# Where a two-stage network meets its second stage: GpSimd's low parts in smaller pieces, a second buffer for words, sums of tokens in half steps

## The chip, the cores and the metric

One core of a Trainium2 chip runs the whole program. The metric is the device time of one execution in microseconds. TensorE (PE), VectorE (DVE), ScalarE (ACT), GpSimd (POOL) and SyncE's DMA queue (SP) work side by side and wait for each other by semaphores.

## The reference

All in float32: `x = attention(q, k, v, p)` over 8 batches of 576 tokens and 512 channels; `x = elu(x @ w_in) @ w_out` with 2048 hidden columns; and last, the part that this case is about:

```python
def _moe2_ref(x, w_a, w_b, w_out):
    a = x @ w_a          # 4608 x 512 by 512 x 1536
    b = x @ w_b
    return (a * b @ w_out).astype(np.float32)
```

The weights arrive as float64 words and are made into float32 on the chip.

## The kernel before, in words

**Numbers.** A float32 product is made of three passes. Each operand is split in a high part (a cast on ACT, L82, L707, L790) and a low part (the operand less its high part, a two-input subtraction: DVE in L83, GpSimd in L708 and L791).

**First phase.** For each batch of 576 tokens PE does 32 steps, `m1_block` (L621): the six matmuls of `l1` (L453) and the twelve of `l2` (L475, two steps behind). Between them `act1` (L459) takes the result through ACT (L461, L462), DVE (L465, the step's `gf`), ACT (L467, high part) and DVE (L469, low part). Other work is put between these instructions at a time counted in half steps: `put(t, fn)` notes it and `run_until` (L517) issues it, at an even time ahead of L465 and at an odd time ahead of L469. T7 is the time at which the last batch begins, so T7 + 34 lies in its 18th step. In this phase PE, DVE and ACT keep the order in which the program is written. `x2_out` (L483) copies a half batch's result from four PSUM banks to two staging tiles (`x2s`, two banks each, one copied by ACT and one by DVE) and stores them to DRAM (L494). It comes after step 17 and after the last step of each batch. The banks are free for the next half's `l2` when they are copied.

**Second phase.** Six groups `g` of 768 tokens, twelve rounds `f` of 128 hidden columns each. By a scheme that needs seven products instead of eight, `l3` (L812) makes seven products of sums of weight blocks (tile `e2`, seven blocks with two parts) with sums of token blocks (tiles `s1` to `s7`) in three PSUM banks A, B, C, in the order A1, B6, C5, A2, B7, C3, B4. Each is six matmuls at L802. B7 waits until DVE has read B6 (L827), B4 until DVE has read B7 (L832). `l4` (L846) then does nine matmuls of the round before. Here only PE keeps the written order; the compiler's scheduler fixes that of the other engines when the program is built.

**The border.** The weight sums of group 0 are made on the spot. `e_load_words` (L690) loads the float32 words of w_a and w_b of one `f` into two tiles with the tag `wmag`, of which there are two, so a new pair waits until the pair before has been read. `e_make` (L696) makes four block sums on DVE (L702 to L705, tile `wc`), casts seven blocks on ACT in three instructions (512, 256 and 1024 columns) and takes seven low parts on GpSimd in three instructions of the same sizes (L708), then stores the tile to DRAM for the other groups (`ed`, L709). `e2` has two buffers, so the ACT casts for `f + 2` start when round `f` is through. `o_load` (L786) loads and splits a block of w_out, with one GpSimd instruction of 512 columns (L791). `x_load` (L717) loads four token tiles with eight DMAs, and `s_steps` (L733) makes the parts s1 to s7 and four sums of 768 columns in eight steps, put at T7 + 45, 47, ... 59. For the later groups the steps come at the end of the group before.

**Buffers.** The pool `stage` has five buffers with the tag `wst`: the token tiles, their sum `x2s1`, the weight sums `wc` and the staging tiles `x2s` all come from them, in the order in which the program asks.

```python
put(T7 + 14, e_make, 0)
put(T7 + 20, e_load_words, 1)
put(T7 + 30, e_make, 1)
put(T7 + 36, e_load_words, 2)
put(T7 + 36, x_load, 0)
for n in range(8):
    put(T7 + 45 + 2 * n, s_step, 0, n)
```

Of the kernel before, what the change touches and what calls it, by code (L numbers as in the profile page):

```python
# [20 lines left out]
P = 128  # L21
# [4 lines left out]
def program(tc, q, k, v, p, w_in, w_out, w_a, w_b, w_out2, out):  # L26
# [21 lines left out]
    HT = 384  # L48
# [12 lines left out]
    with ctx:  # L61
# [628 lines left out]
        def e_load_words(f):  # L690
            for kind in "ab":
                t = stage.tile([P, 512], F32, tag="wmag", name=f"wl{kind}{f}", bufs=2)
                nc.sync.dma_start(t, wf[kind, f])
                wst2[kind, f] = t

        def e_make(f):  # L696
# [9 lines left out]
            for i, n, src in ((0, 2, a.rearrange("p (n x) -> p n x", n=2)), (2, 1, b[:, None, h2]), (3, 4, c)):  # L706
                nc.scalar.copy(e[:, i:i + n, 0, :], src)  # L707
                nc.gpsimd.tensor_tensor(e[:, i:i + n, 1, :], src, e[:, i:i + n, 0, :].bitcast(F32), op=ALU.subtract)  # L708
# [19 lines left out]
        def s_part(g, i, src):  # L728
            s = p2.tile([P, 2, 2 * HT], F32R, tag=f"s{i}", name=f"s{i}_{g}")
            split(s[:, 0, :], s[:, 1, :], src)  # L730
            ss[i] = s.rearrange("p h (k n) -> p h k n", k=2)

        def s_steps(g):  # L733

            flat = lambda t, kh: xs[g, t, kh].rearrange("p k n -> p (k n)")
            tt = nc.vector.tensor_tensor

            def first():
                s_part(g, 1, flat(0, 0))
                xs[g, "s1"] = stage.tile([P, 2 * HT], F32, tag="wst", name=f"x2s1_{g}")  # L740
                tt(xs[g, "s1"], flat(1, 0), flat(1, 1), op=ALU.add)

            def second():
                tt(flat(1, 0), flat(0, 0), flat(1, 0), op=ALU.subtract)
                tt(flat(0, 0), xs[g, "s1"], flat(0, 0), op=ALU.subtract)

            def seventh():
                tt(flat(0, 1), flat(0, 1), flat(0, 0), op=ALU.subtract)
                s_part(g, 3, flat(0, 1))

            return [
                first,
                second,
                lambda: s_part(g, 6, flat(0, 0)),
                lambda: s_part(g, 5, xs[g, "s1"]),
                lambda: s_part(g, 2, flat(0, 1)),
                lambda: s_part(g, 7, flat(1, 0)),
                seventh,
                lambda: s_part(g, 4, flat(1, 1)),
            ]  # L760

        def s_step(g, n):
            if n == 0:
                ss["steps"] = s_steps(g)
            ss["steps"][n]()
# [6 lines left out]
        put(T7 + 36, x_load, 0)  # L772
        for n in range(8):
# [153 lines left out]
```

## Time and profile before

| what | value |
|---|---|
| time, median of 3 runs | 1645.46 us (1644.58 to 1646.12) |
| the profiled execution's own time | 1646.58 us |
| its span, first to last instruction | 1644.8 us |
| mean granted TensorE clock | 0.979 of full speed |
| PE busy | 1569.8 us, 95% of the span |
| DVE busy | 1025.1 us, 62% |
| ACT busy | 717.0 us, 44% |
| POOL busy | 168.8 us, 10% |

In a timeline row the first number is the start from the span's start, the second the time from the start of the first to the end of the last instruction of the row; a bracket gives the idle time of the engine before it and what ended that. An instruction that waits for something after it has been taken up is shown as longer. The last batch's steps lie at about 717 to 799 us, group 0's rounds at 800 to 926 us.

### The profile page before, as it was taken

The page shows a single profiled execution, that of the slowest core. Times are in us where ns is not written, and L with a number is a line of the kernel's source. Part 1 is how long each engine was busy: PE and PEld are TensorE (multiplying, and loading weights), DVE is VectorE, ACT ScalarE, POOL GpSimd, SP SyncE. Part 2 cuts the span into 40 slices and gives each one's busy share as a digit, 9 for nine tenths or more (in the row PEclk, how much of TensorE's full clock was granted, in tenths as well). Part 3 has the DMA queues.
Part 4 walks back from the last instruction along what each step waited for, and adds up shares of the span by engine and source line. Part 5 has one row for each costly group of instructions (what it writes and reads, how often), then busy time and mean ns, then how long its engine had stood idle before and what let it go on. Part 6 is the DMA issues. An engine that isn't in the chain of part 4 may idle for free.

```text
span 1644.8 us, 27465 instructions
## 1 busy us (share of the span) xinstructions
PE 1569.8 (95%) x10824; PEld 1438.4 (87%) x10824; DVE 1025.1 (62%) x2054; ACT 717.0 (44%) x1579; POOL 168.8 (10%) x122
## 2 busy tenths in 40 slices
PE   5488999999999999999889999999999999999999
PEld 3376998989898999999788899989989989998997
DVE  6988676777777676755588735634545453563452
ACT  6675666666666666665433312312222221231211
POOL 3321010000000100011364100000000000000000
PEclk7599999999999999999999999999999999999999
DMA  8755334525262624114366745535445554552541
GB/s 253 179 162 129 105 102 103 131 53 142 76 158 69 154 80 110 47 66 144 117 229 233 268 148 185 221 136 207 180 166 188 213 201 147 184 208 107 211 180 39
DMA packets 214785, 247.95 MB, mean 151 GB/s; under 512 B 150144, under 2 KB 180864, under 8 KB 205440
## 3 DMA queue, kind: packets, MB, share of 16 engines
q1 hardware_dynamic: 214656, 246.19, 46.3%
q8 instruction: 85, 1.39, 0.3%
q14 instruction: 44, 0.36, 0.1%
HBM read 194.64 MB, written 51.51 MB: 150 GB/s over the span
## 4 chain that ended last, share of the span: by engine, by line
PE 79%; DVE 6%; issue 4%; ACT 3%; DMA 3%; POOL 3%; SPq 2%; DVEq 0%; POOLq 0%; ACTq 0%
PE x2a L475 21%; PE o L846 17%; PE B L802 12%; PE h L453 10%; PE C L802 8%; PE A L802 8%; POOL e L708 2%; SPq L164 1%; POOL wo L791 1%; DMA wst_i<-in_moe_w_in_dram 1%; DVE gr L469 1%; DVE gf L465 1%; PE pp L301 1%; ACT gr L467 0%; DVE wr L83 0%
## 5 line engine op out<-in xcount | busy, mean ns | idle before, releaser
L475 PE MATMUL x2a<-gr,wout 128*128 128x288 f32 x3072 | 466.2, 300 | 10.3 <-DVE gr L469 6.4
L475 PEld LDWEIGHTS x2a<-gr,wout 128*128 128x128 f32 x3072 | 424.1, 190 | 51.6 <-issue 12.3
L846 PE MATMUL o<-wo,c 128*128 128x512 f32 x1296 | 309.2, 393 | 0.0
L846 PEld LDWEIGHTS o<-wo,c 128*128 128x128 f32 x1296 | 243.7, 189 | 48.2
L802 PE MATMUL B<-s,e 128*128 128x384 f32 x1296 | 262.8, 337 | 11.1 <-DVE u L827 5.3
L453 PE MATMUL h<-a,wr 128*128 128x288 f32 x1536 | 251.2, 299 | 16.9 <-DVE gf L465 8.6
L453 PEld LDWEIGHTS h<-a,wr 128*128 128x128 f32 x1536 | 220.8, 191 | 26.4 <-DVE gf L465 12.9
L802 PEld LDWEIGHTS B<-s,e 128*128 128x128 f32 x1296 | 228.2, 189 | 15.2 <-DVE u L827 7.8
L802 PE MATMUL A<-s,e 128*128 128x384 f32 x864 | 174.7, 336 | 1.0 <-ACT p L825 1.0
L802 PE MATMUL C<-s,e 128*128 128x384 f32 x864 | 173.9, 335 | 0.0
L465 DVE SCALAR_TENSOR_TENSOR gf<-ge,h 128x288 f32<-128x288 f32 x256 | 113.7, 445 | 85.8 <-ACT ge L462 83.1
L467 ACT CAST gr<-gf 128x288 fp32r<-128x288 f32 x256 | 110.4, 432 | 129.8 <-DVE gf L465 128.7
L802 PEld LDWEIGHTS A<-s,e 128*128 128x128 f32 x864 | 153.8, 188 | 7.2 <-ACT p L825 1.3
L469 DVE TENSOR_TENSOR gr<-gf,gr 128x288 fp32r<-128x288 f32 x256 | 131.5, 514 | 34.4 <-ACT gr L467 32.3
L802 PEld LDWEIGHTS C<-s,e 128*128 128x128 f32 x864 | 152.8, 189 | 0.0
L82 ACT CAST c<-u 128x384 fp32r<-128x384 f32 x72 | 36.8, 512 | 230.3 <-DVE u L835 230.3
L461 ACT ACTIVATE ge<-h 128x288 f32<-128x288 f32 x256 | 104.5, 409 | 74.0 <-PE h L453 73.3
L832 DVE TENSOR_TENSOR v<-p,B 128x384 f32<-128x384 f32 x72 | 39.8, 552 | 143.3 <-PE B L802 143.2
L462 ACT ACTIVATE ge<-ge 128x288 f32<-128x288 f32 x256 | 113.8, 445 | 7.6
L827 DVE TENSOR_TENSOR u<-p,B 128x384 f32<-128x384 f32 x72 | 39.7, 552 | 105.1 <-PE B L802 105.1
L825 ACT COPY p<-A 128x384 f32<-128x384 f32 x72 | 34.7, 482 | 120.2 <-PE A L802 120.1
L829 ACT COPY p<-C 128x384 f32<-128x384 f32 x72 | 34.7, 482 | 102.2 <-PE C L802 102.2
(342 smaller groups left out, 1449.1 us busy)
## 6 DMA issues: line engine op xcount, KB each, us to landing
e<-ed SPq DMA_DIRECT2D x60, 1792.0 KB, 7.1
ed<-e SPq DMA_DIRECT2D x12, 1792.0 KB, 6.4
x2d<-x2s SPq DMA_DIRECT2D x32, 288.0 KB, 2.4
out_dram<-osb SPq DMA_DIRECT2D x36, 256.0 KB, 2.0
v<-in_v_dram SPq DMA_DIRECT2D x8, 1024.0 KB, 7.8
wst_i<-in_moe_w_in_dram SPq DMA_DIRECT2D x16, 512.0 KB, 5.4
wst_o<-in_moe_w_out_dram SPq DMA_DIRECT2D x16, 512.0 KB, 4.5
kst<-in_k_dram SPq DMA_DIRECT2D x112, 72.0 KB, 2.5
```

Of the source, the lines that this page charges most:

```text
L82: nc.scalar.copy(hi, src)
L453: nc.tensor.matmul(t[:, :HS], w[:, wi, o * P:(o + 1) * P], x[:, xi, :], start=(n == 0), stop=(n == 5))
L461: nc.scalar.activation(e, t[:, :HS], AF.Relu, scale=-1.0)
L462: nc.scalar.activation(e, e, AF.Exp, scale=-1.0)
L465: nc.vector.scalar_tensor_tensor(g, e, -1.0, t[:, :HS], op0=ALU.add, op1=ALU.max)
L467: nc.scalar.copy(gr[:, 0, :], g)
L469: nc.vector.tensor_tensor(gr[:, 1, :], g, gr[:, 0, :].bitcast(F32), op=ALU.subtract)
L475: nc.tensor.matmul(acc[d][:, :HS], wout_r[f][:, wi, d * P:(d + 1) * P], gr[:, xi, :], start=(first and n == 0), stop=(last and n == 2),)
L802: nc.tensor.matmul(bank[:, :HT], es[f][:, E_OF[i], wi, k * P:(k + 1) * P], ss[i][:, xi, k, :], start=(first and n == 0), stop=(n == 5), sk ...
L827: nc.vector.tensor_tensor(u, p1, pB, op=ALU.add)
L832: nc.vector.tensor_tensor(v, p1, pB, op=ALU.add)
L846: nc.tensor.matmul(acc, cr[:, xi, t * P:(t + 1) * P], wo[f][:, wi, :], start=(f == 0 and n == 0), stop=(f == NF2 - 1 and n == 2),)
```

## The change

Five edits. (1) `e_make`'s three GpSimd instructions become seven of 256 columns, and `o_load`'s one becomes two of 256. (2) The word pairs of f = 3, 5, 7, 9, 11 go into one tile of the tag `wst` instead of two of `wmag`. (3) Word pairs are asked for a round earlier: pair 3 at T7 + 62, pair f + 4 in round f. (4) `x_load` of group 0 moves from T7 + 36 to T7 + 28. (5) The eight steps on tokens become 22 half steps of 384 columns, one in each half step from T7 + 40 to T7 + 61, in another order of the parts; for the later groups the same 22 stand where the eight stood.

```diff
@@ -688,8 +688,9 @@
         xs, ss = {}, {}
 
         def e_load_words(f):
-            for kind in "ab":
-                t = stage.tile([P, 512], F32, tag="wmag", name=f"wl{kind}{f}", bufs=2)
+            both = stage.tile([P, 2, 512], F32, tag="wst", name=f"wl{f}") if f % 2 and f > 1 else None
+            for n, kind in enumerate("ab"):
+                t = stage.tile([P, 512], F32, tag="wmag", name=f"wl{kind}{f}", bufs=2) if both is None else both[:, n, :]
                 nc.sync.dma_start(t, wf[kind, f])
                 wst2[kind, f] = t
 
@@ -705,7 +706,10 @@
             nc.vector.tensor_tensor(c[:, 3, :], a[:, h2], c[:, 2, :], op=ALU.subtract)
             for i, n, src in ((0, 2, a.rearrange("p (n x) -> p n x", n=2)), (2, 1, b[:, None, h2]), (3, 4, c)):
                 nc.scalar.copy(e[:, i:i + n, 0, :], src)
-                nc.gpsimd.tensor_tensor(e[:, i:i + n, 1, :], src, e[:, i:i + n, 0, :].bitcast(F32), op=ALU.subtract)
+                for x in range(n):
+                    nc.gpsimd.tensor_tensor(
+                        e[:, i + x, 1, :], src[:, x, :], e[:, i + x, 0, :].bitcast(F32), op=ALU.subtract
+                    )
             nc.sync.dma_start(ed[f], e.bitcast(F32))
             es[f] = e
 
@@ -725,43 +729,39 @@
                     done += n
                 xs[g, t, kh] = x
 
-        def s_part(g, i, src):
-            s = p2.tile([P, 2, 2 * HT], F32R, tag=f"s{i}", name=f"s{i}_{g}")
-            split(s[:, 0, :], s[:, 1, :], src)
-            ss[i] = s.rearrange("p h (k n) -> p h k n", k=2)
-
         def s_steps(g):
 
-            flat = lambda t, kh: xs[g, t, kh].rearrange("p k n -> p (k n)")
             tt = nc.vector.tensor_tensor
-
-            def first():
-                s_part(g, 1, flat(0, 0))
-                xs[g, "s1"] = stage.tile([P, 2 * HT], F32, tag="wst", name=f"x2s1_{g}")
-                tt(xs[g, "s1"], flat(1, 0), flat(1, 1), op=ALU.add)
-
-            def second():
-                tt(flat(1, 0), flat(0, 0), flat(1, 0), op=ALU.subtract)
-                tt(flat(0, 0), xs[g, "s1"], flat(0, 0), op=ALU.subtract)
-
-            def seventh():
-                tt(flat(0, 1), flat(0, 1), flat(0, 0), op=ALU.subtract)
-                s_part(g, 3, flat(0, 1))
-
-            return [
-                first,
-                second,
-                lambda: s_part(g, 6, flat(0, 0)),
-                lambda: s_part(g, 5, xs[g, "s1"]),
-                lambda: s_part(g, 2, flat(0, 1)),
-                lambda: s_part(g, 7, flat(1, 0)),
-                seventh,
-                lambda: s_part(g, 4, flat(1, 1)),
-            ]
+            x11, x12, x22, x21 = (xs[g, t, kh] for t, kh in ((0, 0), (0, 1), (1, 1), (1, 0)))
+            s1 = stage.tile([P, 2, HT], F32, tag="wst", name=f"x2s1_{g}")
+            steps = []
+
+            def combine(dst, a, b, op):
+                steps.extend(lambda k=k: tt(dst[:, k, :], a[:, k, :], b[:, k, :], op=op) for k in range(2))
+
+            def part(i, src):
+                ss[i] = p2.tile([P, 2, 2, HT], F32R, tag=f"s{i}", name=f"s{i}_{g}")
+                steps.extend(lambda k=k: split(ss[i][:, 0, k, :], ss[i][:, 1, k, :], src[:, k, :]) for k in range(2))
+
+            part(1, x11)
+            combine(s1, x21, x22, ALU.add)
+            part(5, s1)
+            combine(x21, x11, x21, ALU.subtract)
+            combine(x11, s1, x11, ALU.subtract)
+            part(6, x11)
+            part(7, x21)
+            part(2, x12)
+            combine(x12, x12, x11, ALU.subtract)
+            part(3, x12)
+            part(4, x22)
+            return steps
+
+        NS = 22
 
         def s_step(g, n):
             if n == 0:
                 ss["steps"] = s_steps(g)
+                assert len(ss["steps"]) == NS
             ss["steps"][n]()
 
         put(T7 + 4, e_load_words, 0)
@@ -769,9 +769,10 @@
         put(T7 + 20, e_load_words, 1)
         put(T7 + 30, e_make, 1)
         put(T7 + 36, e_load_words, 2)
-        put(T7 + 36, x_load, 0)
-        for n in range(8):
-            put(T7 + 45 + 2 * n, s_step, 0, n)
+        put(T7 + 28, x_load, 0)
+        for n in range(NS):
+            put(T7 + 40 + n, s_step, 0, n)
+        put(T7 + 62, e_load_words, 3)
         m1_block(B - 1)
         while pend:
             run_pend()
@@ -788,7 +789,8 @@
             nc.sync.dma_start(t, wf["o", f])
             w = p4.tile([P, 2, 512], F32R, tag=f"wo{f}", name=f"wo{f}", bufs=1)
             nc.scalar.copy(w[:, 0, :], t)
-            nc.gpsimd.tensor_tensor(w[:, 1, :], t, w[:, 0, :].bitcast(F32), op=ALU.subtract)
+            for x in (slice(0, 256), slice(256, 512)):
+                nc.gpsimd.tensor_tensor(w[:, 1, x], t[:, x], w[:, 0, x].bitcast(F32), op=ALU.subtract)
             wo[f] = w
 
         def bank2(tag, name, bufs):
@@ -869,8 +871,8 @@
                         o_load(f)
                         if f + 2 < NF2:
                             e_make(f + 2)
-                        if f + 3 < NF2:
-                            e_load_words(f + 3)
+                        if f + 4 < NF2:
+                            e_load_words(f + 4)
                     c1[f], c2[f] = l3(g, f)
                     if g and f + 2 < NF2:
                         e_load(f + 2, g)
@@ -882,7 +884,7 @@
                 if g + 1 < NG:
                     for f in range(2):
                         e_load(f, g + 1)
-                    for n in range(8):
+                    for n in range(NS):
                         s_step(g + 1, n)
                 acc2 = bank2("A", f"o{g}_{TT}", 2)
                 for f in range(NF2 - 1):
```

## Rows read from the trace of the kernel before

**Rows 1.** Page, part 2: busy tenths of PE in 40 equal slices (41 us each).
```profile
PE   5488999999999999999889999999999999999999
```

**Rows 2.** Timeline of PE, 740 to 925 us: start, length, instructions, idle time before.
```profile
759.03 1.88 PE L475 MATMUL x2a<-gr,wout 128*128 128x288 f32 x12 [0.44 <-ACT x2s L492]
...
779.26 1.75 PE L475 MATMUL x2a<-gr,wout 128*128 128x288 f32 x12
...
781.65 0.29 PE L475 MATMUL x2a<-gr,wout 128*128 128x288 f32 x1
782.20 1.75 PE L475 MATMUL x2a<-gr,wout 128*128 128x288 f32 x11 [0.26 <-DVE gr L469]
...
793.88 0.29 PE L475 MATMUL x2a<-gr,wout 128*128 128x288 f32 x1
...
817.83 2.29 PE L802 MATMUL B<-s,e 128*128 128x384 f32 x6 [3.60 <-DVE v L832]
...
823.50 1.20 PE L802 MATMUL A<-s,e 128*128 128x384 f32 x6
...
832.87 1.23 PE L802 MATMUL A<-s,e 128*128 128x384 f32 x6
...
878.52 1.23 PE L802 MATMUL A<-s,e 128*128 128x384 f32 x6
...
883.35 1.31 PE L802 MATMUL B<-s,e 128*128 128x384 f32 x6 [0.47 <-DVE u L827]
...
888.67 1.23 PE L802 MATMUL A<-s,e 128*128 128x384 f32 x6
```

**Rows 3.** Windows: from, to, length, busy of PE, PEld, DVE, ACT, POOL; PEclk, DMA share, GB/s.
```profile
815.00:820.00 5.00, 2.17 (x7) 2.17 (x8) 4.36 (x8) 0.00 (x0) 2.03 (x2) 0.63 1.03 367
...
927.00:955.00 28.00, 28.00 (x125) 23.17 (x124) 9.85 (x15) 4.03 (x7) 0.00 (x0) 1.00 0.45 159
```

**Rows 4.** Timeline of VectorE (DVE), 740 to 925 us, columns as in rows 2.
```profile
780.82 0.96 DVE L83 TENSOR_TENSOR s<-x2s,s 128x768 fp32r<-128x768 f32 x1 [1.24 <-ACT s L82]
...
815.49 0.42 DVE L702 TENSOR_TENSOR wc<-wlb,wla 128x256 f32<-128x256 f32 x1 [3.40 <-DMA wlb<-wfb]
...
879.00 1.15 DVE L83 TENSOR_TENSOR c<-u,c 128x384 fp32r<-128x384 f32 x1 [1.13 <-ACT c L82]
880.07 2.75 DVE L83 TENSOR_TENSOR c<-w,c 128x384 fp32r<-128x384 f32 x1
```

**Rows 5.** Timeline of GpSimd (POOL), 740 to 925 us, columns as in rows 2.
```profile
834.46 2.40 POOL L708 TENSOR_TENSOR e<-wc,e 128x1024 fp32r<-128x1024 f32 x1 [0.57 <-ACT e L707]
...
878.99 0.75 POOL L708 TENSOR_TENSOR e<-wlb,e 128x256 fp32r<-128x256 f32 x1
879.68 2.73 POOL L708 TENSOR_TENSOR e<-wc,e 128x1024 fp32r<-128x1024 f32 x1
```

**Rows 6.** Timeline of ScalarE (ACT), 740 to 925 us, columns as in rows 2.
```profile
779.62 0.43 ACT L467 CAST gr<-gf 128x288 fp32r<-128x288 f32 x1 [0.97 <-DVE gf L465]
779.96 0.83 ACT L82 CAST s<-x2s 128x768 fp32r<-128x768 f32 x1
780.69 0.40 ACT L461 ACTIVATE ge<-h 128x288 f32<-128x288 f32 x1
781.13 0.44 ACT L462 ACTIVATE ge<-ge 128x288 f32<-128x288 f32 x1
...
878.46 0.51 ACT L82 CAST c<-u 128x384 fp32r<-128x384 f32 x1
```

**Rows 7.** Chain that ended last, 740 to 960 us: start, length, what.
```profile
760.84 6.50 DMA x2d<-x2s
```

**Rows 8.** Timeline of SyncE's DMA queue (SP), 740 to 925 us, columns as in rows 2.
```profile
757.56 0.32 SPq L709 DMA_DIRECT2D ed<-e  x1
```

**Rows 9.** Page, part 6: DMA issues, KB each, us to landing.
```profile
ed<-e SPq DMA_DIRECT2D x12, 1792.0 KB, 6.4
x2d<-x2s SPq DMA_DIRECT2D x32, 288.0 KB, 2.4
```

## The prediction

> **What bounds the kernel now.** I read the page first: PE is at 8 or 9 tenths in every slice after the first three, and only slices 19 to 21, some 780 to 900 us, fall off [rows 1]. That is the border which the change touches. PE's timeline then shows how much is lost there. An untroubled step of the first phase takes 781.65 - 779.26 = 2.39 us. From 781.65 to 793.88 four steps take 12.23 us, 2.7 too much, because PE waits for DVE's low part `gr` [rows 2]. An untroubled round of the second phase takes 832.87 - 823.50 = 9.37 us. Rounds 3 to 6 together take 878.52 - 832.87 = 45.65 (8.2 lost), and rounds 7 to 10, of which one is shown, 888.67 - 878.52 = 10.15 each (0.78 each, 3.1 in all) [rows 2]. In round 1 B4 stands 3.60 us, then B4 and nine L846 take 823.50 - 817.83 = 5.67 us. Nine L846 are 9 x 28.00/125 = 2.02 us and a product (9.37 - 2.02)/7 = 1.05 [rows 2, 3], so 2.6 more went: the granted clock there was 0.63, between the levels of 2.4 and 1.2 GHz, after PE had stood still [rows 3]. Round 1 thus lost 6.2 us. Together 20 us are lost that the change could reach.
>
> The rows of DVE and GpSimd say why. GpSimd's subtraction of 1024 columns takes 2.40 us at best. While another one runs, DVE's split of 384 columns takes 2.75 us and ends just after it; the split before, which came 0.01 us after a GpSimd piece of 256 columns, took 1.15 us and ended 0.4 us after that piece [rows 4, 5]. So the two shut each other out for whole instructions, and DVE gets its turn between two GpSimd instructions (the next one then lasts 2.73 instead of 2.40, 0.33 more). That split stands ahead of the read of B6, for which B7 waits [rows 2]. In round 1 DVE stood 3.40 us for words not yet landed [rows 4], with L832 behind it and B4 behind that.
>
> **The change, part by part.**
>
> *Words a round earlier, second buffer.* Pair 3 is in SBUF before round 0, so the 3.40 us on DVE go, and with them the stand of B4 and the slow clock. What is late next is the same read behind sums that meet GpSimd's pieces, some 0.8 us. Round 1 gains 6.2 - 0.8 = **5.4** (bounds 2 and 6.2). Each pair's two DMAs only move a round forward on SP; nothing there waits for them.
>
> *GpSimd in pieces.* A piece of 256 takes 879.68 - 878.99 = 0.70 us from start to start [rows 5], so one tile's seven take 4.9 instead of 0.7 + 2.4 + about 1.25 (a 512 taken between) = 4.35; each turn given to DVE adds 0.33, in all 7.2 us of a round of 9.37. No split now waits 2.4 us, but every DVE instruction with two SBUF inputs that meets the pieces costs 0.70 + 0.33 = 1.0 us. I follow one round from its A1 at 0 with today's order on DVE: the splits of c end at 1.0 and 2.1, B6 is read at 2.9 (B7 needs it at 4.2: its wait of 0.47 goes), the four sums end at 3.8, 4.8, 5.8 and 6.2, and B7 is read at 6.7, where B4 could start at 6.3. The wait moves from B7 to B4: 0.5, with 0.1 of restart 0.6 instead of 0.78. Rounds 7 to 10 gain **0.7**. In rounds 2 to 6 the blocks of w_out come on top, four pieces a round: 11 x 0.70 + 8 x 0.33 = 10.3 us of GpSimd against 9.37, so I take a loss of about 0.9 in rounds 2 to 6, less in the last: 0.8 in round 2, which loses nothing today (**0.8 lost**), and 3.4 in rounds 3 to 6, 8.2 - 3.4 = **4.8 gained**. Bounds for rounds 2 to 10 together: all 11.3 gained, or 5 lost (a rival below). GpSimd itself is not the end: `e2` for f + 2 is done by the middle of round f + 1.
>
> *Half steps.* Today each step carries a cast and a split of 768 columns, both after L467, and DVE's split comes up 0.86 us after its cast [rows 4, 6]; the four steps above took 3.06 us each. With both halves in one step I add up starts: L465 to L467 0.48 (an estimate, half of the 0.96 of rows 4), to the cast 0.34 [rows 6], to L461 0.41 (a little over half of 0.73), to L462 0.44, to the second cast 0.35 (as after L467), to its split 0.54 (a cast of 384 starts at 878.46, its split comes up at 879.00 [rows 4, 6]), to the next L465 0.48: 3.04 us, 0.65 over PE's step. But only 7 of the 11 steps carry parts; the 4 with plain sums need about 1.8 us and give 0.6 back. The lag is at most 2.6 us at the end. Today's eight steps of 3.06 build up 8 x 0.67 = 5.4 and PE loses 2.7, so about 2.7 are swallowed by the work that lies ready ahead of PE. So of 2.7 lost about 0.1 stays: **2.6 gained** (bounds 0 and 2.8).
>
> *Half steps at the five later borders.* Twice as many instructions, 11 x 0.15 us more on DVE for each border (a half taken at 0.55, an estimate a little over half of 0.96 [rows 4]). The matmuls of L846 cover it: PE is busy 28.00 of 28.00 us there and DVE 9.85 [rows 3]. Nothing; without that cover 5 x 1.7 = 8.5 us.
>
> *`x_load` eight half steps earlier.* Its eight DMAs pass pair 2 and the store of e2 for f = 1 on SP, and run while the queue is empty. But the four token tiles now take four of the five `wst` buffers before the weight sums for f = 1 take the fifth, and `x2_out` of step 17 asks for two. The first `x2s` gets the buffer of `wc`; the second must wait until the first has landed in DRAM. Today the order is the other way round: the chain shows the last token tile waiting for just that store, 6.50 us after it left [rows 7]. Behind the second `x2s` stand ACT and DVE, in order, and PE, whose next `l2` already waits 0.44 us for these copies [rows 2]. The store can be issued about 759.6, half a us after PE got its first bank; on the median such a store takes 2.4 us, but the 1.8 MB store of e2 leaves ahead of it (today at 757.56) and takes 6.4 [rows 2, 8, 9]. PE, which would do the third bank's matmuls at 759.9, goes on at 762.5 by the one and about 765.6 by the other. I take **5.5 lost**, nearer the 6.50 of the same store, and for the clock, which fell after 3.60 us of standing, **2.3** (bounds for both: 0, should a buffer be free, and 8.4).
>
> The Trainium skill's page "DMA: Bandwidth & Descriptors" (Queues, rings and completion order) says that each DMA engine takes descriptors in ring order, stores from one issuing engine on one ring. By that rule the small store lands after the large one and the stand is the longer one; without it, it would be 2.6. The chain's 6.50 speaks for the rule, though token loads were ahead of it then too.
>
> **Sum.** 5.4 + 0.7 - 0.8 + 4.8 + 2.6 - 5.5 - 2.3 = 4.9 us less than the profiled execution's 1646.58. The median of the runs is 1.1 lower than that: 1645.46 - 4.9, about 1640.5.
>
> **Rivals.** *A buffer is free after all* (the scheduler lets `x2s` go first): 7.8 us are not lost, 1632.7. The five buffers speak against it; that the scheduler settles who asks first only when the program is built, for it. *Sums ahead of the splits*: words are there a round earlier, so the scheduler may set the four sums where DVE idles before the splits of c, in the midst of GpSimd's pieces. Four sums and two splits at 1.0 each end near 5.3, B6 is read at 5.9, and B7 is 1.8 late in each of rounds 2 to 10: 16.2 against 11.3 lost now. With the other terms, 5.4 + 2.6 - 7.8 - 4.9 = -4.7: **1650**, slower. It decides once three sums stand ahead of the splits (0.7 late, as today); four make it worse. *The pieces are no pieces*: if GpSimd's next piece, which starts 0.05 us before the last ends, kept DVE out, a split would wait for the whole, now 0.6 us longer, train: ten rounds 5.9 us worse than today; 5.4 + 2.6 - 7.8 - 5.9 = -5.7, about 1651. The split that ended between two GpSimd instructions speaks against it [rows 4, 5]. By the Trainium skill's page "SBUF — State Buffer" (Who interferes with whom) issue order decides who blocks; a piece issued early would then keep its place, which is this rival.
>
> **How the numbers follow.** Forecast 0.60, free buffer 0.20, sums ahead 0.14, no pieces 0.06. The forecast's own range, with the bounds of the stand and the rounds, is 1634 to 1646; a measurement tells about 0.2%, 3.3 us, from no change, so of its 0.60 some 0.43 are faster, 0.15 the same and 0.02 slower. The second is faster, the third splits 0.05 the same and 0.09 slower, the fourth 0.01 and 0.05. Faster 0.63, same 0.21, slower 0.16. The range takes in the free buffer and most of the slower cases: 1631 to 1649.
>
> **What would show it.** Right: a stand of PE of some 5 us at the first `l2` after step 17 with ACT's L492 behind a store; no `gr` waits from 780 us on; no 3.4 us before L702 in round 1 and a clock of 1.00 there; DVE's splits of c at or under 1.2 us; B7 without a wait and 0.5 us at B4. Wrong: rounds 7 to 10 at 10.2 us or more (sums first), splits of 3 us (no pieces), or no stand at `x2_out`.

## The result, and the profile after

The changed kernel takes 1655.6 us (median of 4 runs, 1653.89 to 1658.06) where the kernel before, measured beside it, takes 1645.79 (1644.58 to 1648.31). The ratio is 1.0058, with a 95% interval of 1.0045 to 1.007: it is slower, where 1640.5 and faster had been forecast. The profiled execution took 1658.06 us with a span of 1656.3, the longest of the four, and 11.5 us more span than the one of before.

Part 1 and 2 of the page of the changed kernel: busy time of each engine, then 40 slices of 41 us, for [rows 1].

```profile
PE 1575.9 (95%) x10824; PEld 1444.9 (87%) x10824; DVE 1007.6 (61%) x2120; ACT 720.8 (44%) x1621; POOL 180.3 (11%) x182
...
PE   5488999999999999998899999999999999999999
```

VectorE has 17.5 us less to do than before, and yet PE is idle longer. Slice 18 (counted from 0, 745 to 787 us), a 9 before, has become an 8. PE's timeline shows where the time goes: start, length, line, count, idle time before and what ended it, for [rows 2].

```profile
760.61 1.09 PE L475 MATMUL x2a<-gr,wout 128*128 128x288 f32 x6 [0.21 <-ACT x2s L492]
...
767.13 1.81 PE L475 MATMUL x2a<-gr,wout 128*128 128x288 f32 x6 [5.43 <-ACT x2s L492]
768.73 1.65 PE L453 MATMUL h<-a,wr 128*128 128x288 f32 x6
770.17 2.88 PE L475 MATMUL x2a<-gr,wout 128*128 128x288 f32 x12
772.89 0.95 PE L453 MATMUL h<-a,wr 128*128 128x288 f32 x6
...
797.03 1.75 PE L475 MATMUL x2a<-gr,wout 128*128 128x288 f32 x11 [0.34 <-DVE gr L469]
...
802.31 2.04 PE L475 MATMUL x2a<-gr,wout 128*128 128x288 f32 x12 [0.23 <-DVE gr L469]
805.33 3.31 PE L475 MATMUL x2a<-gr,wout 128*128 128x288 f32 x23 [0.98 <-DVE gr L469]
810.11 1.31 PE L804 MATMUL B<-s,e 128*128 128x384 f32 x6 [1.47 <-DVE x2s L493]
...
828.67 2.29 PE L804 MATMUL B<-s,e 128*128 128x384 f32 x6 [4.35 <-DVE v L834]
...
853.01 1.33 PE L804 MATMUL B<-s,e 128*128 128x384 f32 x6 [2.82 <-DVE v L834]
...
874.19 1.58 PE L804 MATMUL B<-s,e 128*128 128x384 f32 x6 [2.10 <-DVE v L834]
...
896.15 1.34 PE L804 MATMUL B<-s,e 128*128 128x384 f32 x6 [1.32 <-DVE v L834]
...
935.05 1.34 PE L804 MATMUL B<-s,e 128*128 128x384 f32 x6 [0.17 <-DVE v L834]
```

Three things stand here. First, the stand behind step 17: PE waits 5.43 us for ACT's copy `x2s`, and then runs slowly (six L453 in 1.65 us, a step later in 0.95). Secondly the waits for `gr` are still there; they have only moved to the phase's end. Thirdly the rounds: no product waits for the read of B6 any more, but B4 now waits for the read of B7 (L834, which was L832), in rounds 1, 3, 5 and 7, and for 1.32 to 4.35 us (and for 0.62 in round 10).

I split the difference of the two spans at three marks of PE's timeline: the first B6, the A1 of round 1 and the A1 of round 11. Before they lie at 800.17, 806.54 and 919.13 us, after at 810.11, 816.46 and 928.48.

| stretch | after less before, us |
|---|---|
| up to the first bank of `l2` behind step 17 (760.61 - 0.21 against 759.03 - 0.44) | +1.8 |
| from there to the third L453 behind it, 775.27 against 765.51 | +7.95 |
| from there to the first B6 | +0.2 |
| round 0 and rounds 1 to 10 | -0.6 |
| from round 11 to the end (727.82 against 725.67) | +2.15 |

They add up to 11.5. The first row lies ahead of the change: the stores ahead of the last batch leave at 722.63 us instead of 720.81, before the first DMA that the change moves (723.48). Two of the runs below that are alike up to there, e1 and e5, stand 3.0 us apart behind step 17 (759.63 and 762.64 us for the store). The rest, 9.7, is close to the difference of the medians, 9.8.

SyncE's queue, ACT's timeline and the chain of waits of the changed kernel tell what ended the stand, for [rows 7] and [rows 8].

```profile
723.48 3.70 SPq L728 DMA_DIRECT2D x2f<-x2d  x7
...
760.15 0.32 SPq L713 DMA_DIRECT2D ed<-e  x1
760.87 0.32 SPq L494 DMA_DIRECT2D x2d<-x2s  x1
...
820.70 0.32 SPq L694 DMA_DIRECT2D wla<-wfa  x1
821.71 0.32 SPq L694 DMA_DIRECT2D wlb<-wfb  x1
```

```profile
766.68 0.40 ACT L492 COPY x2s<-x2a 128x288 f32<-128x288 f32 x1 [6.12 <-DMA x2d<-x2s]
```

```profile
760.87 5.71 DMA x2d<-x2s
```

Seven of the eight token loads (`x2f`) leave at 723.48 us, 34.5 sooner than the first did before (757.97). The program asks for them only eight half steps sooner, some 9.6 us; but in the queue that was built they now stand ahead of two word pairs and two stores `ed`, behind which they stood. They hold four of the five buffers. The first `x2s` gets the fifth once GpSimd has read the weight sums in it, and its store leaves at 760.87; the second copy waits until that store has landed, 5.71 us later, behind the large store `ed` that left 0.72 us ahead of it.

The windows of the changed kernel (from, to, length, busy time of PE, PEld, DVE, ACT, POOL; PEclk, DMA share, GB/s) show the clock behind the two longest waits, for [rows 3]: 0.61, between 2.4 and 1.2 GHz, like the 0.63 of before in round 1.

```profile
768.00:774.00 6.00, 6.00 (x31) 6.00 (x31) 1.72 (x4) 1.83 (x5) 0.00 (x0) 0.61 0.13 49
...
826.00:832.00 6.00, 3.33 (x9) 3.08 (x10) 5.90 (x13) 1.01 (x3) 2.13 (x4) 0.61 0.98 345
```

VectorE's timeline in rounds 1 and 7, for [rows 4] (`wl` holds the words of an odd pair, `wla` and `wlb` those of an even one):

```profile
821.01 0.54 DVE L829 TENSOR_TENSOR u<-p,B 128x384 f32<-128x384 f32 x1
...
825.46 0.96 DVE L703 TENSOR_TENSOR wc<-wlb,wla 128x256 f32<-128x256 f32 x1 [3.36 <-issue]
826.35 0.94 DVE L704 TENSOR_TENSOR wc<-wlb 128x256 f32<-128x256 f32 x1
827.21 0.94 DVE L705 TENSOR_TENSOR wc<-wlb,wc 128x256 f32<-128x256 f32 x1
828.07 0.54 DVE L834 TENSOR_TENSOR v<-p,B 128x384 f32<-128x384 f32 x1
828.54 0.41 DVE L703 TENSOR_TENSOR wc<-wl 128x256 f32<-128x256 f32 x1
...
889.43 1.09 DVE L83 TENSOR_TENSOR c<-w,c 128x384 fp32r<-128x384 f32 x1
890.78 0.55 DVE L829 TENSOR_TENSOR u<-p,B 128x384 f32<-128x384 f32 x1 [0.26 <-PE B L804]
893.20 0.43 DVE L703 TENSOR_TENSOR wc<-wlb,wla 128x256 f32<-128x256 f32 x1 [1.86 <-POOL e L710]
...
895.22 0.42 DVE L705 TENSOR_TENSOR wc<-wl,wc 128x256 f32<-128x256 f32 x1
895.55 0.55 DVE L834 TENSOR_TENSOR v<-p,B 128x384 f32<-128x384 f32 x1
```

The split of c takes 1.09 where it took 2.75: GpSimd's pieces do let VectorE in. But the wait of 3.40 us ahead of the first sum in round 1 has come back as 3.36 us, now ahead of the sums of pair 4. The profile names no releaser for it ("issue"), but the words of pair 4 left at 821.71 us and the sum began 3.75 us later; before, they left at 811.70 and the sum began 3.79 us later. In round 7 seven sums stand ahead of the read of B7, and the first waits 1.86 us. The order of VectorE's rows says why. In round 1 three sums of an even pair (L703, L704, L705) stand between the read of B6 (L829) and that of B7 (L834), and those of an odd pair follow. The scheduler has set the sums of pairs 4 and 5 into round 1, of 6 and 7 into round 3, and so on, two pairs in each odd round up to the seventh, and in all four some of them ahead of the read of B7. The program asks for pair 4's sums only in round 2. So the theory for the experiments was: 8 us are lost behind step 17, for want of a buffer; the rounds gain nothing because VectorE's order changed, and it was the words' buffers that changed it; and the half steps brought nothing.

### The profile page after: what moved, and what is told of

It is laid out like the page before. It is cut to its first block, busy times and chain, and to the rows that moved or that the text cites. A ratio compares the mean times of both kernels' runs of the same rounds, so it can differ in the third digit from the quotient of the medians.

```text
span 1656.3 us, 27647 instructions
## 1 busy us (share of the span) xinstructions
PE 1575.9 (95%) x10824; PEld 1444.9 (87%) x10824; DVE 1007.6 (61%) x2120; ACT 720.8 (44%) x1621; POOL 180.3 (11%) x182
## 4 chain that ended last, share of the span: by engine, by line
PE 75%; DVE 9%; ACT 5%; issue 3%; DMA 3%; POOL 3%; SPq 2%; POOLq 0%; DVEq 0%; ACTq 0%
PE x2a L475 20%; PE o L848 17%; PE B L804 12%; PE h L453 10%; PE A L804 8%; PE C L804 7%; POOL e L710 2%; SPq L164 1%; DVE gf L465 1%; ACT gr L467 1%; DMA wst_i<-in_moe_w_in_dram 1%; DVE wr L83 1%; DVE s L83 1%; ACT ge L462 1%; ACT wr L82 1%
## 5 line engine op out<-in xcount | busy, mean ns | idle before, releaser
L475 PE MATMUL x2a<-gr,wout 128*128 128x288 f32 x3072 | 468.1, 301 | 14.4 <-DVE gr L469 6.4
L475 PEld LDWEIGHTS x2a<-gr,wout 128*128 128x128 f32 x3072 | 426.5, 191 | 54.6 <-ACT x2s L492 12.4
L804 PE MATMUL B<-s,e 128*128 128x384 f32 x1296 | 262.1, 336 | 13.5 <-DVE v L834 12.0
L453 PE MATMUL h<-a,wr 128*128 128x288 f32 x1536 | 254.3, 301 | 16.9 <-DVE gf L465 8.6
L453 PEld LDWEIGHTS h<-a,wr 128*128 128x128 f32 x1536 | 223.6, 193 | 26.6 <-DVE gf L465 12.9
L834 DVE TENSOR_TENSOR v<-p,B 128x384 f32<-128x384 f32 x72 | 39.9, 554 | 152.4 <-PE B L804 152.4
L829 DVE TENSOR_TENSOR u<-p,B 128x384 f32<-128x384 f32 x72 | 39.9, 554 | 100.0 <-PE B L804 99.4
L827 ACT COPY p<-A 128x384 f32<-128x384 f32 x72 | 34.5, 479 | 121.0 <-PE A L804 121.0
L831 ACT COPY p<-C 128x384 f32<-128x384 f32 x72 | 34.5, 479 | 103.4 <-PE C L804 103.4
```

The costliest lines, as they stand in the source:

```text
L453: nc.tensor.matmul(t[:, :HS], w[:, wi, o * P:(o + 1) * P], x[:, xi, :], start=(n == 0), stop=(n == 5))
L475: nc.tensor.matmul(acc[d][:, :HS], wout_r[f][:, wi, d * P:(d + 1) * P], gr[:, xi, :], start=(first and n == 0), stop=(last and n == 2),)
L804: nc.tensor.matmul(bank[:, :HT], es[f][:, E_OF[i], wi, k * P:(k + 1) * P], ss[i][:, xi, k, :], start=(first and n == 0), stop=(n == 5), sk ...
L829: nc.vector.tensor_tensor(u, p1, pB, op=ALU.add)
L834: nc.vector.tensor_tensor(v, p1, pB, op=ALU.add)
```

## The experiments

The table gives each run's time, its ratio to the kernel before on the same chip, and what the trace of its profiled execution shows at the marks used above: the first B6; what rounds 1 to 10 take over 10 x 9.37 us; and the stretch from round 11 to the end.

| run | median, us | ratio (95%) | first B6 | rounds 1 to 10 lose | from round 11 |
|---|---|---|---|---|---|
| before | 1645.8 to 1647.9 | 1 | 800.17 | 18.9 | 725.67 |
| after | 1655.6 | 1.0058 (1.0045 to 1.007) | 810.11 | 18.3 | 727.82 |
| e1 late token tile | 1647.9 | 1.0002 (0.9994 to 1.0011) | 800.37 | 17.7 | 727.81 |
| e2 words back | 1653.33 | 1.0041 (1.0027 to 1.0054) | 808.66 | 13.2 | 728.47 |
| e3 whole low parts | 1656.3 | 1.0053 (1.004 to 1.0066) | 808.19 | 18.7 | 727.75 |
| e4 steps back | 1647.66 | 1.0003 (0.9994 to 1.0011) | 801.22 | 17.9 | 725.64 |
| e5 = e1 + e2 | 1644.11 | 0.9978 (0.9969 to 0.9987) | 802.65 | 13.5 | 728.38 |
| e8 VectorE by hand | 1646.79 | 0.9999 (0.999 to 1.0008) | 799.25 | 17.0 | 727.43 |
| e9 e8, words back | 1649.38 | 1.0009 (1.0 to 1.0018) | 799.33 | 20.6 | 727.40 |
| e10 e8, whole low parts | 1658.27 | 1.0064 (1.0052 to 1.0077) | 800.61 | 28.8 | 727.45 |
| e11 sums first | 1642.92 | 0.9975 (0.9965 to 0.9985) | 800.60 | 11.8 | 727.37 |
| e12 e11, whole low parts | 1645.94 | 0.999 (0.998 to 1.0) | 802.89 | 15.0 | 727.51 |
| e13 e11, words back | 1651.6 | 1.0029 (1.0018 to 1.0041) | 801.21 | 23.9 | 727.45 |
| e14 e11, steps sooner | 1640.69 | 0.9964 (0.9951 to 0.9976) | 799.68 | 11.8 | 727.38 |

The kernel before took 1645.79 us beside the changed kernel, 1647.29 beside e1 to e4, 1647.36 beside e5 to e10 and 1647.89 beside e11 to e14. A difference between the changed kernel and a later run is therefore uncertain by some 2 us.

### The stand: one token tile later

```diff
-        def x_load(g):
-            for t, kh in ((0, 0), (0, 1), (1, 1), (1, 0)):
+        def x_load(g, parts=((0, 0), (0, 1), (1, 1), (1, 0))):
+            for t, kh in parts:
...
-        put(T7 + 28, x_load, 0)
+        put(T7 + 28, x_load, 0, ((0, 0), (1, 1), (1, 0)))
+        put(T7 + 36, x_load, 0, ((0, 1),))
```

> The changed kernel, but the load of the token tile (0,1), which is the last that the half steps need, is issued at half step T7+36 instead of T7+28, behind the three others, so that a wst buffer is left for the second x2s copy. Theory (four token tiles in four of five wst buffers make x2_out of step 17 wait for its own store): the 5.4 us stand of PE at the first l2 and the slow clock behind it (about 2.5 us) go, x2_out is as quick as before; span some 8 us under the changed kernel's, about 1647, level with the kernel before. Rival (the stand is the store queue's, whatever the buffers; or the lag is only moved to the half steps): the stand stays or comes back as waits of PE for gr, time within 2 us of the changed kernel, 1654 to 1657.

It took 1647.9 us, 7.7 less (9.2 less, if each is taken against the kernel before beside it), and the stand is gone: the twelve L475 of the first `l2` run without a break. From PE's timeline of this run:

```profile
759.01 1.88 PE L475 MATMUL x2a<-gr,wout 128*128 128x288 f32 x12
...
795.56 3.34 PE L475 MATMUL x2a<-gr,wout 128*128 128x288 f32 x23 [0.97 <-DVE gr L469]
800.37 1.31 PE L805 MATMUL B<-s,e 128*128 128x384 f32 x6 [1.47 <-DVE x2s L493]
...
819.12 2.29 PE L805 MATMUL B<-s,e 128*128 128x384 f32 x6 [4.66 <-DVE v L835]
```

From the first L475 behind step 17 to the first B6 this run takes 41.4 us and the changed kernel 49.5: one buffer at that moment is worth 8 us. The rest is as in the changed kernel, the wait of B4 in round 1 among it, which is 4.66 here.

### The half steps: eight steps again

```diff
-        NS = 22
+        NS = 8
...
-        put(T7 + 28, x_load, 0)
+        put(T7 + 36, x_load, 0)
...
-            put(T7 + 40 + n, s_step, 0, n)
+            put(T7 + 45 + 2 * n, s_step, 0, n)
```

The old functions of the eight steps are back with it.

> The changed kernel with the token sums as before: eight steps at T7+45 and on, and the four token loads at T7+36. Theory (the stand at x2_out comes from the early token loads, and the half steps gained nothing): no stand, the steps take 3.06 us each again and PE loses about 2.7 us there, border rounds as in the changed kernel; some 8 us under the changed kernel's, 1645 to 1648, level with the kernel before. Rival (half steps were worth the 2.6 us forecast, and the stand 5.4): 3 to 5 us under it, 1651 to 1653.

It took 1647.66 us, as the theory had it. Between this run and e1 the steps differ, and with them the time of three token loads, and the medians agree: half steps are worth nothing as they stand. The traces show two amounts of opposite sign. From the store `ed` of that place (758.91 in e1, 758.83 here) to the first B6 e1 is 0.9 us quicker. From round 11 on it is 2.2 us slower, and so is every run with half steps, by 1.7 us or more, while this run and the kernel before agree within 0.03. The windows of both from 930 to 1640 us show it (columns as above), first this run, then the changed kernel:

```profile
930.00:1640.00 710.00, 710.00 (x3708) 660.76 (x3707) 336.04 (x608) 151.87 (x289) 0.00 (x0) 1.00 0.48 174
```

```profile
930.00:1640.00 710.00, 709.17 (x3706) 659.95 (x3705) 347.82 (x672) 160.21 (x331) 0.00 (x0) 1.00 0.48 176
```

PE never stands with the eight steps. With half steps it waits at B4 in the last round of each group but the last (0.17 us at 935.05 above). VectorE's timeline of the changed kernel shows a half step ahead of the read of B6:

```profile
930.70 0.56 DVE L83 TENSOR_TENSOR s<-x2f,s 128x384 fp32r<-128x384 f32 x1 [1.39 <-ACT s L82]
931.17 0.55 DVE L829 TENSOR_TENSOR u<-p,B 128x384 f32<-128x384 f32 x1
```

That read begins 2.69 us after the round's A1 (928.48), in the kernel before 2.37 (921.50 after 919.13). From it to the read of B7 it is then 3.28 us with six half instructions between, where three whole ones took 3.21. So the read of B7 is 0.4 us later, and 0.3 of that arises ahead of the read of B6. With what is lost around the wait this makes 2.15/5 = 0.43 us for each of five borders.

### Words and pieces, with the scheduler's order

```diff
-            both = stage.tile([P, 2, 512], F32, tag="wst", name=f"wl{f}") if f % 2 and f > 1 else None
...
-        put(T7 + 62, e_load_words, 3)
...
-                        if f + 4 < NF2:
-                            e_load_words(f + 4)
+                        if f + 3 < NF2:
+                            e_load_words(f + 3)
```

> The changed kernel with the words of the weight pairs loaded as in the kernel before: one pair of buffers, f + 3 in every round, none at T7+62. Theory (in odd rounds DVE has the weight sums of two pairs ahead of the read of B7, since the even pair's words still come late and the odd pair's early): every round has four sums again; the waits of B4 in rounds 3, 5 and 7 (2.8, 2.1 and 1.3 us) fall to 0.6 or less each, round 1 stays 6 us or more late; span about 3 us (1.5 to 5) under the changed kernel's. Rival (the second buffer does help, what is slow is DVE's pieces): rounds 3 to 7 no better, round 1 worse, time 0 to 4 us above the changed kernel's.

It took 1653.33 us, 2.3 less than the changed kernel (3.8 less, each against the kernel before beside it), as expected, though not as told: round 1 loses 1.4 us instead of 8.6, round 2 4.9 instead of nothing, round 3 nothing instead of 3.1. The rounds lose 13.2 us instead of 18.3 in these two executions (the shortest of this run's and the longest of the changed kernel's), so that edits 2 and 3 by themselves cost the rounds 2 to 5 us. B6's wait for `x2s` is 0.79 again, not 1.47: the sums of pair 3 had come between the last two copies. Each round has the sums of one pair again, and VectorE's timeline has the read of B7 ahead of them in rounds 1 to 4, behind all or most of them from round 5 on.

```diff
-                for x in range(n):
-                    nc.gpsimd.tensor_tensor(
-                        e[:, i + x, 1, :], src[:, x, :], e[:, i + x, 0, :].bitcast(F32), op=ALU.subtract
-                    )
+                nc.gpsimd.tensor_tensor(e[:, i:i + n, 1, :], src, e[:, i:i + n, 0, :].bitcast(F32), op=ALU.subtract)
```

The same is done for the blocks of w_out.

> The changed kernel with GpSimd's low parts unsplit, as in the kernel before (three instructions for a pair, one for a block of w_out). Theory (the pieces do let DVE in): the splits of c wait up to 2.75 us again and B7 waits in most rounds; the time is 3 to 8 us above the changed kernel's, 1659 to 1664. Rival (the pieces give nothing, since each DVE instruction that meets them pays for it): within 2 us of the changed kernel's. Second rival (more, smaller pieces hold DVE up more often): 2 to 6 us below it.

It took 1656.3 us, level with the changed kernel: the theory missed, and the first rival held as far as the time goes. Yet the split of c shows the pieces at work. Groups of VectorE's instructions from 805 to 920 us, by form (busy time, mean ns of one, idle before), first whole low parts, then the changed kernel:

```profile
L83 DVE TENSOR_TENSOR c<-w,c 128x384 fp32r<-128x384 f32 x10 | 21.0, 2097 | 0.0
```

```profile
L83 DVE TENSOR_TENSOR c<-w,c 128x384 fp32r<-128x384 f32 x10 | 10.5, 1046 | 0.0
L703 DVE TENSOR_TENSOR wc<-wlb,wla 128x256 f32<-128x256 f32 x5 | 3.5, 692 | 8.9 <-POOL e L710 3.5 <-issue 3.4 <-DMA wlb<-wfb 2.0
```

The pieces halve the split, and in the changed kernel what they free is spent again: VectorE stands 8.9 us ahead of the first sum of the even pairs. But this pair of runs does not price the pieces alone, for the scheduler's order moved with them. By VectorE's timeline of e3 the read of B7 stands ahead of all sums in rounds 1 and 3 and behind all eight in rounds 5 and 7. What the pieces are worth in one and the same order is seen only further down, where the order is fixed by hand.

> The run with the late token tile, with the words of the weight pairs back as in the kernel before too (one pair of buffers, f + 3, none at T7+62); pieces and half steps stay. Theory (the words' second buffer lets the scheduler put the sums of two pairs ahead of the read of B7, and costs what the run with the words back alone gave, 2.3 us): 1647.9 - 2.3, about 1645.5 (1643.5 to 1647), 0.1% under the kernel before. Rival (that gain came from the early part, where runs differ by 2 us): level with the run with the late token tile, 1647 to 1649.

This run has both edits, of e1 and e2. It took 1644.11 us, 3.8 under e1 and 0.22% under the kernel before: edits 1, 4 and 5 with the token tile mended gain 3 us. As the half steps are worth nothing, this should be the pieces'; that is inferred, since no run here takes the pieces out of this one. By their VectorE timelines, every run with the scheduler's order that has edits 2 and 3 (the changed kernel, e1, e3, e4) makes the sums of two pairs in odd rounds, and none without them does (the kernel before, e2, e5). So it is the words that change the order.

### VectorE's order by hand

```diff
+        order.close()
         with order:
+            order.enter_context(tc.manual_schedule(engines={ET.PE, ET.DVE}))
...
-                            e_make(f + 2)
...
-                    c1[f], c2[f] = l3(g, f)
+                            e_make(f + 2, late)
+                    c1[f], c2[f], todo = l3(g, f, todo + late[:2], late[2:])
```

`late` holds the four sums and what follows them, `todo` the two splits; `l3` issues its third argument after the read of B6 and its fourth at its end. The next word pair is asked for behind `l3`, not ahead of it. The order of ScalarE and GpSimd stays the scheduler's.

> The run with the late token tile, with VectorE in program order in the twelve rounds of group 0: after the read of B6 the splits of the c tiles of the round before and two weight sums of pair f + 2, then the reads of B7, C, A and B4, then the two other sums. Nothing else is changed. Theory (the order of DVE that the scheduler chose, two pairs' sums ahead of the read of B7 in odd rounds, keeps PE waiting 4.7, 2.8, 2.1, 1.3 and 0.6 us at B4, with 4.5 us of slow clock and restart; the engines themselves have room): those waits go, rounds 1 to 10 lose 6 us or less instead of some 18; 9 to 14 us under the run with the late token tile, 1634 to 1639. Rival (pieces, sums and splits shut each other out for more than the round has, whatever the order): PE waits as long at other banks, C or B4 of every round; 1644 to 1649.

It took 1646.79 us, within 1.1 us of e1. The wait of 4.66 us in round 1 is gone, but rounds 1 to 9 now lose 1.5 to 2.4 each, 17.0 with round 10: the rival's picture. VectorE's timeline in round 4 shows how:

```profile
843.75 0.55 DVE L846 TENSOR_TENSOR u<-p,B 128x384 f32<-128x384 f32 x1 [1.49 <-ACT p L844]
844.23 1.13 DVE L83 TENSOR_TENSOR c<-u,c 128x384 fp32r<-128x384 f32 x1
845.28 1.09 DVE L83 TENSOR_TENSOR c<-w,c 128x384 fp32r<-128x384 f32 x1
846.29 0.96 DVE L704 TENSOR_TENSOR wc<-wlb,wla 128x256 f32<-128x256 f32 x1
847.17 0.94 DVE L705 TENSOR_TENSOR wc<-wlb 128x256 f32<-128x256 f32 x1
848.04 0.54 DVE L853 TENSOR_TENSOR v<-p,B 128x384 f32<-128x384 f32 x1
```

Four instructions of about 1 us, twice what they take alone, stand between the reads of B6 and B7, where e1 in a round without sums has 2.50 us of idle time. And ACT is late with its copy of A1, because the cast of `wc` stands ahead of it and waits for the last sum:

```profile
842.29 1.05 ACT L721 CAST e<-wc 128x1024 fp32r<-128x1024 f32 x1 [0.73 <-DVE wc L707]
843.25 0.47 ACT L844 COPY p<-A 128x384 f32<-128x384 f32 x1
```

> The run with VectorE by hand, with GpSimd's low parts whole, as in the kernel before. Theory (the pieces let DVE in, and it was only the order that hid it): splits and sums wait up to 2.75 us each again, 3 to 8 us over the run by hand. Rival (the pieces are worth nothing here either, as in the pair of runs with the scheduler's order, 1655.6 and 1656.3): within 1.5 us of it.

1658.27 us, 11.5 over e8: theory, not rival, and more than expected. In this order of VectorE, the same in both runs, the pieces are worth 11.5 us.

> The run with VectorE by hand, with the words as in the kernel before (one pair of buffers, f + 3). Theory (with the order by hand a sum stands behind words that land only some 5 us after GpSimd has read the pair before, and the reads of the banks stand behind that sum): 3 to 10 us over the run by hand. Rival (the sums of pair f + 2 come so late by hand that the words are there in both): within 1.5 us of it; the second buffer is then worth nothing.

1649.38 us, 2.6 over e8, just under the theory's range, and above the rival's.

The next version takes all four sums before the read of B7 and only one split, so that GpSimd gets its last four blocks sooner:

```diff
-c1[f], c2[f], todo = l3(g, f, todo + late[:2], late[2:])
+c1[f], c2[f], todo = l3(g, f, todo[:1] + late[:4], todo[1:] + late[4:])
```

> The run with VectorE by hand, with another order by hand: after the read of B6 one split of the c tiles (c1) and all four weight sums, then the reads of the other banks, then the split of c2. Theory (in the run by hand four instructions of 0.95 to 1.1 us stand ahead of the read of B7, and the cast of the sums waits on ScalarE for the last sum with the copy of A1 behind it, 2.3 us a round; with the sums done early GpSimd is through with a pair sooner and the sums meet no pieces, 0.4 us each): rounds of 9.4 to 10.2 us instead of 10.9 to 11.7, 8 to 18 us under the run by hand, 1629 to 1639. Rival (five instructions ahead of the read of B7 meet the pieces all the same, 5 us where there are 2.9): PE waits longer at B4, 1650 to 1660.

1642.92 us, 3.9 under e8, in the theory's direction and half the least that it named. Rounds 6 to 10 lose 0.52 us each or less. In rounds 3 to 5, while GpSimd still does the blocks of w_out, the sums meet pieces all the same (0.96 us each) and B4 waits 1.2 us.

> The run with the sums first, with GpSimd's low parts whole. Theory (pieces matter once the order leaves DVE free to use the turns): 3 to 12 us over the run with the sums first, as by hand, where it was 11.5. Rival (they matter only where sums and splits meet GpSimd's instructions, and these now meet few): within 2 us.

1645.94 us, 3.0 over e11: the pieces are worth 3 us here, the lower end of what the theory said.

> The run with the sums first, with the words as in the kernel before (one pair of buffers, f + 3). Theory (the four sums of pair f + 2 now come early in round f, and its words can only be asked for when GpSimd has read pair f + 1, late in round f - 1 or early in f; DVE waits for them with the read of B7 behind): 3 to 15 us over the run with the sums first; this is what the second buffer is for. Rival (the words are there in time): within 1.5 us.

1651.6 us, 8.7 over e11. The first sum of round 1 waits 3.75 us for the words. VectorE's timeline of this run:

```profile
817.28 0.56 DVE L703 TENSOR_TENSOR wc<-wlb,wla 128x256 f32<-128x256 f32 x1 [3.75 <-DMA wlb<-wfb]
```

So the second buffer, which costs 2.3 and 3.8 us (e2, e5) where the scheduler chooses the order anew, gains 8.7 us in this one.

### The half steps, three half steps sooner

```diff
-            put(T7 + 40 + n, s_step, 0, n)
+            put(T7 + 37 + n, s_step, 0, n)
```

> The run with the sums first, with the 22 half steps begun three half steps sooner (T7+37). Theory (each half step still takes ScalarE and VectorE longer than PE's 2.38 us, and what lags is paid where the phase ends, because no work lies behind it; with three free half steps at the end the lag is caught up): the waits for gr and x2s from 785 to 800 us, 2.1 us in the run by hand, fall to 1 or less; 1 to 2 us under the run with the sums first. Rival (the lag comes from the last half steps alone, whatever went before): the same time within 0.5 us.

1640.69 us, 2.2 under e11 and 0.36% under the kernel before, the lowest median here (its interval overlaps that of e11). From its timeline of PE:

```profile
783.94 1.73 PE L475 MATMUL x2a<-gr,wout 128*128 128x288 f32 x11 [0.38 <-DVE gr L469]
...
791.78 1.72 PE L475 MATMUL x2a<-gr,wout 128*128 128x288 f32 x11 [0.35 <-DVE gr L469]
...
799.68 1.31 PE L817 MATMUL B<-s,e 128*128 128x384 f32 x6 [0.55 <-DVE x2s L493]
```

The waits of the tail have fallen to 0.38 + 0.35 + 0.55 = 1.28 us, from 2.09 in e11 (0.34, 0.23, 0.97, 0.55). The theory had them at 1 or less. From the first L475 behind step 17 (760.13 in e11, 760.44 here) to the first B6 this run is 1.2 us quicker, and the two profiled spans differ by 1.0; the theory's 1 to 2 us stand, and what the medians have beyond that is no more than runs differ by.

## Why the prediction was wrong, step by step

**Two readings ahead of the sum were off.** In [rows 1] only slices 19 and 20, 781 to 863 us, fall to 8 behind the start, not 19 to 21. And round 1 of the kernel before lost 7.6 us, not 6.2: PE also waited 1.01 us ahead of its A2, at 810.84.

**The stand at `x2_out`: right.** Forecast 5.5 lost and 2.3 for the clock, 7.8 together; measured 7.95, of which the longer wait is 5.43 + 0.21 - 0.44 = 5.20 and the rest, 2.75, goes with the slow clock. Two small errors cancel in the sum. The store took 5.71 us behind the large one, not the median of 2.4. The Trainium skill's page "DMA: Bandwidth & Descriptors" (Queues, rings and completion order) has descriptors taken in ring order; the trace agrees, as the small store, issued 0.72 us after the large one, took 5.71 us, near the longer of the two prices. The rival of a free buffer is out, and e1 shows that a free buffer is what it takes.

**Round 1: wrong by 6.4.** The failed step is "Pair 3 is in SBUF before round 0, so the 3.40 us on DVE go". Pair 3's sums did move ahead of round 0, to between the last copies `x2s`. What came after them in VectorE's order was not asked. I kept "today's order on DVE" with four sums a round; the scheduler chose another once the words' buffers had changed, with pairs 4 and 5 in round 1, and pair 4 shares its buffer with pair 2 as before: its words leave at 820.70 and 821.71, once GpSimd has read pair 2, and the sums wait for them. Round 1 lost 7.6 and now loses 8.6: a loss of 1.0 where 5.4 had been gained. In e2, with the old buffers, the read of B7 stands ahead of the sums in round 1, and the round loses 1.4.

**Rounds 2 to 10: gain 1.5 where 4.7 stood.** The sum is 4.8 + 0.7 - 0.8; measured are 11.3 lost before and 9.8 after. The half of it that rests on the pieces held: splits of 1.05 us, no wait at B7, nothing lost in rounds 2, 4, 6, 8 and 9. What failed is again the order: the sums of two pairs fall together in rounds 1, 3, 5 and 7, and B4 waits 2.82, 2.10 and 1.32 us in three of them where I had 0.5 in each round. The rival *sums ahead of the splits*, with a chance of 0.14, came nearest: the scheduler did move the sums, but to another place, behind the splits and ahead of the read of B7. *The pieces are no pieces* is refuted by the splits. The Trainium skill's page "SBUF — State Buffer" (Summary: rules for kernel authors) says that, where VectorE has two inputs in SBUF and GpSimd reads SBUF, the second to issue blocks until the first is through. The trace agrees, with a piece as the first, not the row of pieces: the split takes 1.05 us, while four pieces in a row take 2.82 (`wo` at 812.40).

**Half steps: 2.6 forecast, -0.2 measured.** By e1 and e4 the half steps gained 0.9; by e5, with the words' buffers of the kernel before, they gained 0.5 (762.00 to 802.65 us, against 759.03 to 800.17). The words took 0.7 back: B6 waits 1.47 instead of 0.80 behind the last copies. The step that failed is that a lag "at most 2.6 us at the end" is swallowed "by the work that lies ready ahead of PE": it falls due just where the phase ends and no work lies ready any more (0.34, 0.23 and 0.98 us). e14 shows it from the other side: ended three half steps sooner, they are 1.2 us cheaper by the trace.

**Half steps at the later borders: "nothing" was -2.15.** "The matmuls of L846 cover it" looked at PE's work after round 11, where it holds. Not covered was round 11 itself: its reads of B6 and B7 stand among the half-step instructions on the same engine, the read of B7 comes 0.4 us later than with whole steps, and PE waits 0.17 us for it. The cover was right for the data and wrong for the queue.

Of the signs named, the stand, the splits and B7 came as told; the `gr` waits, the wait ahead of the first sum of round 1 and its clock did not, nor the 0.5 us at B4 of every round.

Together: 7.95 + 0.2 + 2.15 - 0.6 = 9.7 us lost, where 4.9 had been gained. Nearly half of the gap of 14.6 is round 1, a fifth each are the other rounds and the tail, the rest the later borders. Of the 10.1 us that rounds 1 to 10 were to gain (5.4 + 4.7), the best order by hand gains 7.1 (e11: 18.9 less 11.8 lost), the scheduler's 0.6. So by these traces the order accounts for 6.5 of the 9.5 missing; whether another order would give the other 3.0 was not tried.

What stays open: why the scheduler takes pairs two at a time is not known, and no run has edit 2 without edit 3, so that the second buffer and the earlier loads are not told apart as its cause. A second buffer for the even pairs as well, with the scheduler's own order, was not tried either, nor the eight steps at the later borders of the fastest version, which by the last column of the table (727.38 against 725.64) should be worth 1.7 us.

## What to carry to other kernels

Where a scheduler fixes an engine's order, a change of buffers is also a change of that order: price it by the order in the program that is built, not by the old trace with a wait taken out. An instruction that frees a bank should not stand behind one that waits for a load; e2 to e13 show the second buffer worth -3.8 or -2.3 us where the scheduler orders VectorE anew, and +2.6 and +8.7 in two orders by hand; the pieces are worth 11.5 and 3.0 us in those two orders, and nothing in e3, where the order moved with them. And before a load is moved forward, count the pool's buffers at the place it moves past.

## What the runs showed of the hardware

- A subtraction of two SBUF tiles on VectorE takes 1.04 to 1.13 us (384 columns) or 0.94 to 0.96 (256) where it meets GpSimd's pieces in full, and 0.55 or 0.42 alone; one that reads a PSUM bank takes 0.54 to 0.56 either way. So pieces of 256 columns cost such an instruction about 0.5 us at either length, which makes many short sums dearer than few long ones.
- A wait of PE of 0.17 us at B4 stands in a border that is 0.43 us longer; the product behind it shows 1.31 to 1.34 us instead of 1.22.
- Two half steps of 384 columns take VectorE 1.02 us, one of 768 takes 0.95; I had allowed twice this difference.
